# FNet mixing into a sigmoid-gated FFN: the first batch's transform grows with its rows, the Nyquist column travels as row 0 of G2, and weight conversions move within their iterations

## The chip, the cores and the metric

The kernel runs on one core of one Trainium2 chip. The metric is the device time of a whole execution in microseconds. Five engines work side by side, each with its own instruction stream in program order: TensorE (PE, with PEld for the loading of its stationary operand), VectorE (DVE), ScalarE (ACT), GpSimd (POOL) and SyncE (SP). SyncE is used to issue DMAs; ScalarE issues some as well, and an issue takes its turn among the engine's other instructions.

## The reference

An input x of 8 batches, 3008 rows and 256 features goes through a two-dimensional Fourier transform, of which the real part is kept. The result, seen as 24064 tokens of 256 features, goes through a gated feed-forward layer of 1536 hidden units.

```python
X = np.fft.fft(np.fft.fft(x, axis=1), axis=2).real      # (8, 3008, 256)
x = X.reshape(24064, 256)
gate = 1.0 / (1.0 + np.exp(-(x @ w_gate)))              # (256, 1536)
val = x @ w_val                                         # (256, 1536)
out = (gate * val) @ w_out                              # (1536, 256)
```

## The kernel before, in words

**Symmetry.** The host sends each batch as four groups of 126 x 6 rows (a row, its mirror, the row half a turn away and the mirror of that). `fold_ops` adds and subtracts these groups and mirrored features, so that a transform along the rows needs only cosine and sine tables `st` for a quarter of the frequencies, and one along the features only 128 columns. Batch 0 is folded on VectorE, the others on GpSimd, a few operations per iteration.

**Transform along the rows.** `half` sums, for one of two parities `blk` and one kind `what`, over the six row slices q: even q into a PSUM bank `ev`, odd q into `od`. ScalarE copies `ev` to `a`, and VectorE forms a + od and a - od, which go to places k and M - k of a row block. The kinds are pk (what 0, cosine part of features 0 to 127), qk (what 1, sine part of features 1 to 127) and ek (what 2, the feature 128, spread over all partitions). Batch 0 computes its own ek from a stationary operand `we`, which ScalarE fills with 128 copies of one column. For batches 1 to 7 the column comes by `e_load` (seven DMAs of x8), `e_fold`, `e_rows` and a trip through DRAM.

**Transform along the features.** It is merged into the weights. `merge` multiplies the table `dt` (256 x 256) with 256 columns of w_gate (g = 0) or w_val (g = 1): `ps` gives G1 (cosine rows) and G2 (127 sine rows), `pe` gives the column for feature 128, turned so that hidden units lie on partitions (`ge`). The weights are 64 bit floats; `weight_round` makes 32 bit floats of the raw words in six steps (L163 and L164 on ScalarE, L165, L166 and L168 on VectorE, L170 on GpSimd). Conversions are staged through `jobs`, numbered j; the first KEEP = 5 come ahead of the loop, the others three per two iterations. `forms` prepares w_out as seven combinations per pair of hidden blocks, a product of two by two blocks with seven multiplications.

**Main loop.** Frequencies 0 to 1504 are cut in 6 chunks of up to 256. For each batch, chunk and pair i of hidden blocks (6 pairs of 2 x 128) there are two iterations. In each, `front` computes pa (G1 x pk) and pb (G2 x qk) for gate and value, VectorE adds ge x ek to pa (ae, L326), and z = ae + pb and ae - pb (L329, L330) are the values at k and at its mirror. ScalarE applies the sigmoid (L495), `gate` multiplies gate and value (h, L341), GpSimd makes the sums sf (L343 to L347), and `back` does the second matrix product into four banks po, two pairs later. After the last pair of a chunk `finish` evacuates and stores through SyncE. An iteration ends with one entry of `later` and the entries of `side` (`at`, `split`): weight work in iterations 0 to 9, loads of the next batch, folds, row transforms.

**Order around the change.** The emission order is the order on each engine. An iteration emits front, gate of the iteration before, back, sigmoid, then the side work, in which `merge` comes ahead of `weight_round`. PSUM has eight banks: four in the rotating pool x (pa, pb, ps, pe, ev, od) and four for po. The raw words of the first five weights share three buffers; later ones lie in `mega`, in the place of batch 0's rows.

Of the kernel before, what the change touches and what calls it, by code (L numbers as in the profile page):

```python
# [38 lines left out]
NQ = 6  # L39
# [5 lines left out]
def kernel(  # L45
# [45 lines left out]
    def mm(o, l, r, start, stop):  # L91
        nc.tensor.matmul(o, l, r, start=start, stop=stop, skip_group_check=True)  # L92

    def bank(name):
        return psx.tile([P, 512], F32, name=name, tag="x")


# [7 lines left out]

    def load_x(b, nq):
        X[b] = xp.tile([NP, 4, NQ, D], F32, name="x4", tag="x4")
        for q in range(0, NQ, nq):
            rows(X[b][:, :, q : q + nq], xf[b, :, :, q : q + nq])

    dt = const.tile([P, 2, D], F32, name="dt")
    st = const.tile([NP, 2, NQ, NE + NO], F32, name="st")
    wf = const.tile([P, NPR, 7, P], F32, name="wf")
    G1 = const.tile([P, 2, F], F32, name="G1")
    G2 = const.tile([HD - 1, 2, F], F32, name="G2")
    ge = const.tile([P, 2, NFT], F32, name="ge")

    x8 = const.tile([NP, B - 1, 4, NQ], F32, name="x8")
    ed = dram.tile([B - 1, NK], F32, name="ed")

    def load_tables():
        for t in range(2):
            for cs in (slice(0, NE), slice(NE, NE + NO)):
                rows(st[:, t, :, cs], stab[:, t, :, cs])


    jobs = [(w, c) for c in range(NPR) for w in range(3)]
    RAW, WS = {}, {}
    mega = []
    KEEP = 5  # L130
# [21 lines left out]
            RAW[j] = raw  # L152
            nc.sync.dma_start(out=raw.rearrange("p c f w -> p c (f w)"), in_=src.bitcast(I32))

    def weight_round(j):
        if j not in RAW:
            return
        raw = RAW.pop(j)
        lo, hi = raw[:, :, :, 0], raw[:, :, :, 1]
        ws = WS[j]  # L160
        wi = ws.bitcast(I32)
        ts = nc.vector.tensor_scalar
        nc.scalar.activation(ws, hi.bitcast(F32), AF.Abs)  # L163
        nc.scalar.activation(lo, lo.bitcast(U32), AF.Copy, scale=2.0 ** -29)  # L164
        ts(out=ws, in0=ws, scalar1=2.0 ** -15, scalar2=HUGE, op0=ALU.max, op1=ALU.min)  # L165
        ts(out=wi, in0=wi, scalar1=3, scalar2=0x3FFFFFF8, op0=ALU.logical_shift_left,  # L166
           op1=ALU.bitwise_and)
# [4 lines left out]
    def weight_use(j):  # L172
        w, c = jobs[j]
        (forms(WS.pop(j), c) if w == 2 else merge(WS.pop(j), w, c))
# [31 lines left out]
    def fold_ops(b, eng, nq):  # L206
        x4 = X.pop(b)
        tt = eng.tensor_tensor
        ops = []

        def point(i, j, q):
            tt(x4[:, i, q, 1:D], x4[:, i, q, 1:D], x4[:, j, q, D - 1 : 0 : -1], op=ALU.add)

        def first(i, j, q):
            tt(x4[:, i, q, 0], x4[:, i, q, 0], x4[:, j, q, 0], op=ALU.add)

        def feat(v, r, q):
# [12 lines left out]
        if b:  # L230

            for n, group in enumerate(zip(*[kind(q) for q in qs])):
                ops += [f for fs in group for f in fs]
                if n < 2:
                    ops.append(lambda n=n: first(2 * n, 2 * n + 1, slice(0, NQ)))
        else:

            for q in qs:
                for n, fs in enumerate(kind(q)):
                    ops += fs  # L240
                    if n < 2:
                        ops.append(lambda n=n, q=q: first(2 * n, 2 * n + 1, q))
# [12 lines left out]
    def half(w, d, blk, sn, rows):  # L255

        c0, n = ((0, NE), (NE, NO))[blk]
        ev, od = bank("ev")[0:rows, 0:n], bank("od")[0:rows, 0:n]
        for o, par in ((ev, 0), (od, 1)):
            for q in range(par, NQ, 2):  # L260
                mm(o, w(q), st[:, int(sn), q, c0 : c0 + n], q == par, q >= NQ - 2)
        a = evp.tile([P, NE], F32, name="a", tag="a")[0:rows, 0:n]
        nc.scalar.copy(a, ev)
# [7 lines left out]
        return then  # L271

    def seq_start(b):
        PQE[b] = (pqp.tile([P, NK], F32, name="pk", tag="pk"),
                  pqp.tile([HD - 1, NK], F32, name="qk", tag="qk"),
                  pqp.tile([P, NK], F32, name="ek", tag="ek"))
        if b:
            nc.sync.dma_start(out=PQE[b][2], in_=ed[b - 1 : b, :].to_broadcast([P, NK]))

    def seq_group(b, blk, what):  # L280
        return half(lambda q: W[b, blk][what][:, q, :], PQE[b][what], blk, what == 1,
                    HD - 1 if what == 1 else P)


    ER = []

    def e_load():
        for b in range(1, B):
            nc.scalar.dma_start(out=x8[:, b - 1], in_=xf[b, :, :, :, HD : HD + 1])
# [8 lines left out]
    def e_rows(blk):  # L298
        if not blk:
            ER.append(cp.tile([B - 1, NK], F32, name="er", tag="c7"))  # L300
        return half(lambda q: x8[:, :, 1 + 2 * blk, q], ER[0], blk, False, B - 1)

    def e_out():
        nc.scalar.dma_start(out=ed, in_=ER.pop())
# [162 lines left out]
    at(i0 + 1, lambda: load_x(1, 3), e_load)  # L467

    for b in range(B - 1):
        s0 = b * per  # L470
        if b:
            at(s0 + 1, lambda b=b: load_x(b + 1, 3))
        f0, g0, gs = (s0 + 9, s0 + 36, 8) if b else (i0 + 9, i0 + 36, 7)

        def folds(f0=f0, b=b):
# [12 lines left out]
    for i in range(2 * len(pairs)):  # L488
# [69 lines left out]
```

## Time and profile before

| What | Value |
|---|---|
| Time, median of 3 runs | 2076.5 us (2075.3 to 2077.08) |
| Span of the profiled execution | 2072.8 us |
| PE busy, share of the span | 2023.2 us, 98% |
| DVE, POOL, ACT busy | 1750.4, 1316.3, 502.2 us |
| First main-loop matmul (pa) | 49.38 us |
| First ae on VectorE | 57.05 us |
| PE busy from 160 to 2063 us | 1902.25 of 1903 us |
| DMA in all | 70.96 MB, of it 0.39 MB in 21552 packets on ScalarE's queue |

Times in a profile count from the first instruction. Busy time of an engine is the sum of its instructions; the rest is waiting. Matmuls in 32 bit floats appear as two records each, so "pa x4" is two products of 128 x 128 by 256. A row of the chain of waits names the instruction that was running when nothing else could have ended the program earlier; a row of order of time has start, duration, engine, line, operation, output and inputs, and in brackets how long the engine had been idle and what released it. The granted clock is that of TensorE, 1.00 for full speed.

### The profile page before, as it was taken

How to read it: one execution, taken by the hardware profiler on the slowest of the kernel's cores; microseconds unless marked ns; L12 is line 12 of the kernel's file. 1: busy time of each engine (PE TensorE's matmuls, PEld its weight loads, DVE VectorE, ACT ScalarE, POOL GpSimd, SP SyncE). 2: the span in 40 equal slices, each digit the busy share in tenths (PEclk: the TensorE clock that was granted, in tenths of full speed). 3: DMA queues.
4: the chain of work that ended last, by engine and by line, in shares of the span. 5: the costliest groups of instructions: out<-in, count | busy, mean ns of one | idle time of the engine just before them, and what ended most of it. 6: DMA issues, size and time to landing. Idle time of an engine off the chain costs nothing.

```text
span 2072.8 us, 27549 instructions
## 1 busy us (share of the span) xinstructions
PE 2023.2 (98%) x9264; PEld 1757.7 (85%) x9264; DVE 1750.4 (84%) x3233; ACT 502.2 (24%) x892; POOL 1316.3 (64%) x1627
## 2 busy tenths in 40 slices
PE   7789999999999999999999999999999999999998
PEld 4677789888898888988899888988889888898887
DVE  4768878998889977998789987899879988798887
ACT  2422222222222222222222222222222222222222
POOL 0546944696558944687556974579545885565654
PEclk9899999999999999999999999999999999999999
DMA  8341000300020100301003000120003010000001
GB/s 207 109 82 12 11 27 16 75 26 11 18 69 14 32 16 11 71 19 27 11 11 80 26 11 11 32 58 26 16 16 71 13 32 11 11 16 15 11 16 24
DMA packets 142281, 70.96 MB, mean 34 GB/s; under 512 B 124783, under 2 KB 128063, under 8 KB 142142
## 3 DMA queue, kind: packets, MB, share of 16 engines
q1 hardware_dynamic: 120590, 68.83, 14.0%
q10 hardware_dynamic: 21552, 0.39, 0.7%
q8 instruction: 74, 1.21, 0.2%
q14 instruction: 65, 0.53, 0.1%
HBM read 44.50 MB, written 24.68 MB: 33 GB/s over the span
## 4 chain that ended last, share of the span: by engine, by line
PE 72%; POOL 14%; DVE 6%; issue 2%; ACTq 1%; ACT 0%; DVEq 0%; POOLq 0%
PE po L92 31%; PE pa L92 18%; PE pb L92 17%; PE ev L92 3%; PE od L92 3%; POOL sf L346 2%; POOL sf L345 2%; POOL sf L343 2%; POOL sf L347 2%; DVE ae L326 2%; DVE h L341 1%; POOL x L218 1%; POOL x L226 1%; POOL x L219 1%; DVE z L330 1%
## 5 line engine op out<-in xcount | busy, mean ns | idle before, releaser
L495 ACT ACTIVATE z<-z 128x512 f32<-128x512 f32 (+1 forms) x576 | 358.5, 622 | 1330.6 <-DVE z L330 1330.6
L326 DVE SCALAR_TENSOR_TENSOR ae<-ek,ge,pa 128x256 f32<-128x256 f32 (+1 forms) x1152 | 489.9, 466 | 194.1 <-PE pa L92 191.0
L92 PE MATMUL pa<-pk,G 128*128 128x256 f32 (+1 forms) x2304 | 587.4, 377 | 9.9 <-ACT G L187 5.2
L92 PE MATMUL pb<-qk,G 127*128 127x256 f32 (+1 forms) x2304 | 585.6, 376 | 0.4 <-DVE z L330 0.4
L92 PE MATMUL po<-sf,wf 128*128 128x256 f32 (+1 forms) x2304 | 537.4, 375 | 0.6
L92 PEld LDWEIGHTS pa<-pk,G 128*128 128x128 f32 x2304 | 438.2, 191 | 69.1 <-ACT G L187 7.4
L92 PEld LDWEIGHTS pb<-qk,G 127*128 127x128 f32 x2304 | 439.0, 191 | 53.2 <-PE pa L92 0.7
L92 PEld LDWEIGHTS po<-sf,wf 128*128 128x128 f32 x2304 | 435.5, 190 | 55.7 <-POOL sf L347 3.5
L345 POOL TENSOR_TENSOR sf<-h 128x256 f32<-128x256 f32 (+1 forms) x288 | 212.6, 738 | 400.0 <-DVE h L341 400.0
L341 DVE TENSOR_TENSOR h<-z 128x512 f32<-128x512 f32 (+1 forms) x576 | 447.0, 776 | 11.4 <-ACT z L495 11.4
L329 DVE TENSOR_TENSOR z<-ae,pb 128x512 f32<-128x512 f32 (+1 forms) x576 | 390.1, 677 | 61.1 <-DVE ae L326 1.4
L92 PE MATMUL po<-h,wf 128*128 128x256 f32 (+1 forms) x1728 | 416.4, 377 | 8.8 <-ACT c L370 8.8
L330 DVE TENSOR_TENSOR z<-ae,pb 128x512 f32<-128x512 f32 (+1 forms) x576 | 386.3, 671 | 0.0
L92 PEld LDWEIGHTS po<-h,wf 128*128 128x128 f32 x1728 | 329.6, 191 | 49.0 <-ACT c L370 9.2
L343 POOL TENSOR_TENSOR sf<-h 128x256 f32<-128x256 f32 (+1 forms) x288 | 219.0, 760 | 225.5 <-DVE h L341 222.3
L346 POOL TENSOR_TENSOR sf<-sf,h 128x256 f32<-128x256 f32 (+1 forms) x288 | 214.6, 745 | 22.6
L347 POOL TENSOR_TENSOR sf<-h,sf 128x256 f32<-128x256 f32 (+1 forms) x288 | 213.5, 741 | 22.6
L382 ACT COPY c<-po 128x512 f32<-128x512 f32 (+1 forms) x144 | 78.4, 580 | 64.4 <-PE po L92 64.3
L389 DVE STREAM_TRANSPOSE os<-c 128x256 f32<-128x256 f32 x192 | 83.8, 438 | 0.0
L92 PE MATMUL ev<-st,x 126*128 126x377 f32 (+5 forms) x204 | 71.9, 489 | 6.0 <-ACT ge L189 6.0
L411 POOL TENSOR_TENSOR c<-c 128x512 f32<-128x512 f32 (+1 forms) x47 | 73.6, 1566 | 0.0
L92 PE MATMUL od<-st,x 126*128 126x377 f32 (+5 forms) x204 | 70.1, 479 | 0.0
(80 smaller groups left out, 745.1 us busy)
## 6 DMA issues: line engine op xcount, KB each, us to landing
x<-in_xf_dram SPq DMA_DIRECT2D x14, 1344.0 KB
out_dram<-os SPq DMA_DIRECT2D x288, 64.0 KB
out_dram<-os SPq DMA_DIRECT2D x96, 56.0 KB
ek<-ed SPq DMA_DIRECT2D x7, 752.5 KB
x<-in_xf_dram SPq DMA_DIRECT2D x3, 896.0 KB
mega<-in_moe_w_out_dram SPq DMA_DIRECT2D x5, 512.0 KB
x<-in_xf_dram SPq DMA_DIRECT2D x14, 168.0 KB
mega<-in_moe_w_gate_dram SPq DMA_DIRECT2D x4, 512.0 KB
```

What stands on the lines that cost most here:

```text
L92: nc.tensor.matmul(o, l, r, start=start, stop=stop, skip_group_check=True)
L326: nc.vector.scalar_tensor_tensor(out=ae[:, g], in0=ek[:, ks], scalar=ge[:, g, f : f + 1], in1=pa[:, g], op0=ALU.mult, op1=ALU.add)
L329: nc.vector.tensor_tensor(z[:, :, 0], ae, pb, op=ALU.add)
L330: nc.vector.tensor_tensor(z[:, :, 1, ::-1], ae, pb, op=ALU.subtract)
L341: nc.vector.tensor_tensor(h[:, fh], z[:, 0], z[:, 1], op=ALU.mult)
L343: tt(s[:, 2], h[:, 0, 0], h[:, 0, 1], op=ALU.subtract)
L345: tt(s[:, 0], h[:, 0, 1], h[:, 1, 1], op=ALU.add)
L346: tt(s[:, 1], s[:, 0], h[:, 0, 0], op=ALU.subtract)
L347: tt(s[:, 3], h[:, 1, 0], s[:, 1], op=ALU.subtract)
L382: nc.scalar.copy(t[:, 2 * j : 2 * j + 2, 0:n], PO[j][:, :, 0:n])
L389: nc.vector.transpose(os_[:, s, 0:nb, h, :], t[:, slot, 0 : nb * TB])
L495: nc.scalar.activation(z[:, 0], z[:, 0], AF.Sigmoid)
```

## The change

The change has these parts.

- Batch 0's rows and the cosine table arrive in alternating slices of two q; weights and the sine table come after them. Each slice is folded, and then its share of four cosine groups is summed; these groups hold eight PSUM banks at once, four of them the po banks. `half` therefore gives back its summing, its copy and its placing apart.
- The column for feature 128 becomes row 0 of G2: `merge` uses 128 rows of the table for its second half. A DMA turns this row of 128 hidden units into a column of `ge`. So that row 0 adds nothing to pb, row 0 of qk must be zero; `feat` sets its source to zero.
- `we` goes; a broadcast view of the column is the stationary operand.
- A conversion is cut in two: `weight_parts` (ScalarE) ahead of the iteration's sigmoid, `weight_join` (VectorE, GpSimd) in the side work. The order of `jobs` changes, so that w_out's part for a pair comes later, and the merges of g = 0 and g = 1 take one iteration each, with one and two conversions beside them.
- `e_load` issues from SyncE.

```diff
--- before.py
+++ after.py
-    def bank(name):
+    def bank(name, other=None):
+        if other is not None:
+            return pso.tile([P, 512], F32, name=name, tag=f"po{other}")
         return psx.tile([P, 512], F32, name=name, tag="x")
...
     def load_x(b, nq):
         X[b] = xp.tile([NP, 4, NQ, D], F32, name="x4", tag="x4")
-        for q in range(0, NQ, nq):
-            rows(X[b][:, :, q : q + nq], xf[b, :, :, q : q + nq])
+        return [lambda q=q: rows(X[b][:, :, q : q + nq], xf[b, :, :, q : q + nq])
+                for q in range(0, NQ, nq)]
...
-    G2 = const.tile([HD - 1, 2, F], F32, name="G2")
+    G2 = const.tile([P, 2, F], F32, name="G2")
...
-    def load_tables():
-        for t in range(2):
-            for cs in (slice(0, NE), slice(NE, NE + NO)):
-                rows(st[:, t, :, cs], stab[:, t, :, cs])
+    def load_table(t, nq):
+        return [lambda q=q: rows(st[:, t, q : q + nq], stab[:, t, q : q + nq])
+                for q in range(0, NQ, nq)]
...
-    jobs = [(w, c) for c in range(NPR) for w in range(3)]
+    jobs = [(w, c - (w == 2)) for c in range(NPR + 1) for w in range(3)
+            if (c if w == 2 else c < NPR)]
...
-    def weight_round(j):
+    def weight_parts(j):
+        if j in RAW:
+            raw, ws = RAW[j], WS[j]
+            lo, hi = raw[:, :, :, 0], raw[:, :, :, 1]
+            nc.scalar.activation(ws, hi.bitcast(F32), AF.Abs)
+            nc.scalar.activation(lo, lo.bitcast(U32), AF.Copy, scale=2.0 ** -29)
+
+    def weight_join(j):
...
-        nc.scalar.activation(ws, hi.bitcast(F32), AF.Abs)
-        nc.scalar.activation(lo, lo.bitcast(U32), AF.Copy, scale=2.0 ** -29)
         ts(out=ws, in0=ws, scalar1=2.0 ** -15, scalar2=HUGE, op0=ALU.max, op1=ALU.min)
...
-    def merge(ws, g, c):
+    def merge(ws, g, c, other):
         cs = slice(c * WC, (c + 1) * WC)
-        ps, pe = bank("ps"), bank("pe")
-        for t in range(2):
-            mm(ps[:, 0:WC], dt[:, t, 0:HD], ws[:, t, :], t == 0, t == 1)
-        for t in range(2):
-            mm(ps[0 : HD - 1, WC : 2 * WC], dt[:, t, HD + 1 : D], ws[:, t, :], False, t == 1)
-        for i in range(WC // P):
+        ps = bank("ps", other)
+        for h in range(2):
             for t in range(2):
-                mm(pe[:, i : i + 1], ws[:, t, i * P : (i + 1) * P], dt[:, t, HD : HD + 1],
-                   t == 0, t == 1)
+                mm(ps[:, h * WC : (h + 1) * WC], dt[:, t, h * HD : (h + 1) * HD], ws[:, t, :],
+                   h == 0 and t == 0, t == 1)
+        nc.scalar.copy(G2[:, g, cs], ps[:, WC : 2 * WC])
         nc.scalar.copy(G1[:, g, cs], ps[:, 0:WC])
-        nc.scalar.copy(G2[:, g, cs], ps[0 : HD - 1, WC : 2 * WC])
-        nc.scalar.copy(ge[:, g, c * WC // P : (c + 1) * WC // P], pe[:, 0 : WC // P])
+        for f in range(c * WC // P, (c + 1) * WC // P):
+            (nc.sync if c else nc.scalar).dma_start(
+                out=ge[:, g, f : f + 1], in_=G2[0:1, g, f * P : (f + 1) * P])
...
         def feat(v, r, q):
-            tt(r[:, q, 0 : HD - 1], v[:, q, 1:HD], v[:, q, D - 1 : HD : -1], op=ALU.subtract)
+            eng.memset(r[:, q, 0:1], 0.0)
+            tt(r[:, q, 1:HD], v[:, q, 1:HD], v[:, q, D - 1 : HD : -1], op=ALU.subtract)
...
-            W[b, blk] = (v[:, :, 0:HD], r[:, :, 0 : HD - 1])
-            if b == 0:
-                we = cp.tile([NP, NQ, P], F32, name="we", tag="c7")
-                ops.append(lambda we=we, v=v: nc.scalar.copy(
-                    we, v[:, :, HD : HD + 1].to_broadcast([NP, NQ, P])))
-                W[b, blk] += (we,)
+            W[b, blk] = (v[:, :, 0:HD], r[:, :, 0:HD],
+                         v[:, :, HD : HD + 1].to_broadcast([NP, NQ, P]))
...
     def e_load():
         for b in range(1, B):
-            nc.scalar.dma_start(out=x8[:, b - 1], in_=xf[b, :, :, :, HD : HD + 1])
+            nc.sync.dma_start(out=x8[:, b - 1], in_=xf[b, :, :, :, HD : HD + 1])
...
+    for fx, ft in zip(load_x(0, 2), load_table(0, 2)):
+        fx()
+        ft()
     for j in range(2):
         weight_load(j)
-    load_x(0, 2)
-    load_tables()
+    for f in load_table(1, 2):
+        f()
     for j in range(2, KEEP):
         weight_load(j)
-    for j in range(2):
-        weight_round(j)
-    for f in fold_ops(0, nc.vector, 2):
+    seq_start(0)
+    folds0 = fold_ops(0, nc.vector, 2)
+    cos = [seq_group(0, blk, what, (2 * blk, 2 * blk + 1) if what else None)
+           for what in (0, 2) for blk in range(2)]
+    for i, f in enumerate(folds0):
         f()
-    for j in range(2):
-        weight_use(j)
-    seq_start(0)
-    for blk, what in ((0, 0), (0, 2), (1, 0), (1, 2), (0, 1), (1, 1)):
-        seq_group(0, blk, what)()
+        for sums, _ in cos:
+            sums(2 * i, 2 * i + 1)
+    weight_parts(0)
+    cos[0][1]()()
+    weight_parts(1)
+    weight_join(0)
+    cos[1][1]()()
+    weight_join(1)
+    for _, then in cos[2:]:
+        then()()
+    sin = [seq_group(0, blk, 1) for blk in range(2)]
+    for i in range(NQ // 2):
+        for sums, _ in sin:
+            sums(2 * i, 2 * i + 1)
+        if i < 2:
+            weight_use(i, i)
     for j in range(2, KEEP):
-        weight_round(j)
-    weight_use(2)
+        weight_parts(j)
+    for _, then in sin:
+        then()()
+    for j in range(2, KEEP):
+        weight_join(j)
...
-    def weight_step(j):
-        weight_round(j)
-        if j + 3 < len(jobs):
-            weight_load(j + 3)
+    def weight_step(i, *js):
+        for j in js:
+            pre.setdefault(i, []).append(lambda j=j: weight_parts(j))
+            at(i, lambda j=j: weight_join(j))
+            if j + 3 < len(jobs):
+                at(i, lambda j=j: weight_load(j + 3))
+    pre = {}
     for c in range(1, NPR):
         i = 2 * (c - 1)
-        at(i, lambda c=c: weight_use(3 * c), lambda c=c: weight_step(3 * c + 2))
-        at(i + 1, lambda c=c: weight_use(3 * c + 1), lambda c=c: weight_use(3 * c + 2))
+        j = 3 * c - 1
+        at(i, lambda j=j: weight_use(j))
+        at(i + 1, lambda j=j: weight_use(j + 1))
+        at(i + (c > 1), lambda j=j: weight_use(j + 2))
         if c + 1 < NPR:
-            at(i, lambda c=c: weight_step(3 * c + 3))
-            at(i + 1, lambda c=c: weight_step(3 * c + 4))
+            weight_step(i, j + 3)
+            weight_step(i + 1, j + 4, j + 5)
+        else:
+            weight_step(i, j + 3)
+            at(i + 1, lambda j=j: weight_use(j + 3))
...
         if i >= 4:
             back(i // 2 - 2, i % 2)
+        for f in pre.pop(i, []):
+            f()
         z = fresh[2]
         nc.scalar.activation(z[:, 0], z[:, 0], AF.Sigmoid)
```

More of the change, by code (lines that the diff above doesn't have):

```diff
@@ L153, in weight_load @@
             nc.sync.dma_start(out=raw.rearrange("p c f w -> p c (f w)"), in_=src.bitcast(I32))
-    def weight_round(j):
+    def weight_parts(j):
[5 more added lines that the diff above has]
+    def weight_join(j):
         if j not in RAW:
             return
-        raw = RAW.pop(j)
+        raw, ws = RAW.pop(j), WS[j]
         lo, hi = raw[:, :, :, 0], raw[:, :, :, 1]
-        ws = WS[j]
         wi = ws.bitcast(I32)
         ts = nc.vector.tensor_scalar
-        nc.scalar.activation(ws, hi.bitcast(F32), AF.Abs)
-        nc.scalar.activation(lo, lo.bitcast(U32), AF.Copy, scale=2.0 ** -29)
         ts(out=ws, in0=ws, scalar1=2.0 ** -15, scalar2=HUGE, op0=ALU.max, op1=ALU.min)
@@ L170, in weight_round, with weight_use @@
         nc.gpsimd.tensor_tensor(wi, wi, lo, op=ALU.add)
-    def weight_use(j):
+    def weight_use(j, other=None):
         w, c = jobs[j]
-        (forms(WS.pop(j), c) if w == 2 else merge(WS.pop(j), w, c))
-    def merge(ws, g, c):
-        cs = slice(c * WC, (c + 1) * WC)
-        ps, pe = bank("ps"), bank("pe")
-        for t in range(2):
-            mm(ps[:, 0:WC], dt[:, t, 0:HD], ws[:, t, :], t == 0, t == 1)
-        for t in range(2):
-            mm(ps[0 : HD - 1, WC : 2 * WC], dt[:, t, HD + 1 : D], ws[:, t, :], False, t == 1)
-        for i in range(WC // P):
+        if w == 2:
+            forms(WS.pop(j), c)
+        else:
+            merge(WS.pop(j), w, c, other)
+    def merge(ws, g, c, other):
+        cs = slice(c * WC, (c + 1) * WC)
+        ps = bank("ps", other)
+        for h in range(2):
             for t in range(2):
-                mm(pe[:, i : i + 1], ws[:, t, i * P : (i + 1) * P], dt[:, t, HD : HD + 1],
-                   t == 0, t == 1)
+                mm(ps[:, h * WC : (h + 1) * WC], dt[:, t, h * HD : (h + 1) * HD], ws[:, t, :],
+                   h == 0 and t == 0, t == 1)
+        nc.scalar.copy(G2[:, g, cs], ps[:, WC : 2 * WC])
         nc.scalar.copy(G1[:, g, cs], ps[:, 0:WC])
-        nc.scalar.copy(G2[:, g, cs], ps[0 : HD - 1, WC : 2 * WC])
-        nc.scalar.copy(ge[:, g, c * WC // P : (c + 1) * WC // P], pe[:, 0 : WC // P])
+        for f in range(c * WC // P, (c + 1) * WC // P):
+            (nc.sync if c else nc.scalar).dma_start(
+                out=ge[:, g, f : f + 1], in_=G2[0:1, g, f * P : (f + 1) * P])
     def forms(ws, c):
@@ L238, in fold_ops, with half, sums, places @@
             for q in qs:
+                part = []
                 for n, fs in enumerate(kind(q)):
-                    ops += fs
+                    part += fs
                     if n < 2:
-                        ops.append(lambda n=n, q=q: first(2 * n, 2 * n + 1, q))
+                        part.append(lambda n=n, q=q: first(2 * n, 2 * n + 1, q))
+                ops.append(lambda part=part: [f() for f in part])
         for blk, (v, r) in enumerate(parts):
-            W[b, blk] = (v[:, :, 0:HD], r[:, :, 0 : HD - 1])
-            if b == 0:
-                we = cp.tile([NP, NQ, P], F32, name="we", tag="c7")
-                ops.append(lambda we=we, v=v: nc.scalar.copy(
-                    we, v[:, :, HD : HD + 1].to_broadcast([NP, NQ, P])))
-                W[b, blk] += (we,)
+            W[b, blk] = (v[:, :, 0:HD], r[:, :, 0:HD],
+                         v[:, :, HD : HD + 1].to_broadcast([NP, NQ, P]))
         return ops
     PQE = {}
-    def half(w, d, blk, sn, rows):
+    def half(w, d, blk, sn, rows, other=None):
         c0, n = ((0, NE), (NE, NO))[blk]
[L258 to L263, printed above, removed]
+        ev, od = [bank(name, other and other[i])[0:rows, 0:n] for i, name in enumerate(("ev", "od"))]
+        def sums(*qs):
+            for q in sorted(qs, key=lambda q: q % 2):
+                mm((ev, od)[q % 2], w(q), st[:, int(sn), q, c0 : c0 + n], q < 2, q >= NQ - 2)
         def then():
+            a = evp.tile([P, NE], F32, name="a", tag="a")[0:rows, 0:n]
+            nc.scalar.copy(a, ev)
+            return lambda: places(a)
+        def places(a):
             nc.vector.tensor_tensor(d[:, blk : blk + 2 * n - 1 : 2], a, od, op=ALU.add)
@@ L270, in then, with whole @@
                                     op=ALU.subtract)
-        return then
+        return sums, then
+    def whole(sums, then):
+        sums(*range(NQ))
+        return then()
     def seq_start(b):
         PQE[b] = (pqp.tile([P, NK], F32, name="pk", tag="pk"),
-                  pqp.tile([HD - 1, NK], F32, name="qk", tag="qk"),
+                  pqp.tile([P, NK], F32, name="qk", tag="qk"),
                   pqp.tile([P, NK], F32, name="ek", tag="ek"))
@@ L278, in seq_start, with seq_group @@
             nc.sync.dma_start(out=PQE[b][2], in_=ed[b - 1 : b, :].to_broadcast([P, NK]))
-    def seq_group(b, blk, what):
-        return half(lambda q: W[b, blk][what][:, q, :], PQE[b][what], blk, what == 1,
-                    HD - 1 if what == 1 else P)
+    def seq_group(b, blk, what, other=None):
+        return half(lambda q: W[b, blk][what][:, q, :], PQE[b][what], blk, what == 1, P, other)
     ER = []
@@ L300, in e_rows @@
             ER.append(cp.tile([B - 1, NK], F32, name="er", tag="c7"))
-        return half(lambda q: x8[:, :, 1 + 2 * blk, q], ER[0], blk, False, B - 1)
+        return whole(*half(lambda q: x8[:, :, 1 + 2 * blk, q], ER[0], blk, False, B - 1))
     def e_out():
@@ L452, in split @@
         at(i, lambda: at(i + 1, f(*args)))
-    def weight_step(j):
-        weight_round(j)
-        if j + 3 < len(jobs):
-            weight_load(j + 3)
+    def weight_step(i, *js):
[5 more added lines that the diff above has]
+    pre = {}
     for c in range(1, NPR):
         i = 2 * (c - 1)
-        at(i, lambda c=c: weight_use(3 * c), lambda c=c: weight_step(3 * c + 2))
-        at(i + 1, lambda c=c: weight_use(3 * c + 1), lambda c=c: weight_use(3 * c + 2))
+        j = 3 * c - 1
+        at(i, lambda j=j: weight_use(j))
+        at(i + 1, lambda j=j: weight_use(j + 1))
+        at(i + (c > 1), lambda j=j: weight_use(j + 2))
         if c + 1 < NPR:
-            at(i, lambda c=c: weight_step(3 * c + 3))
-            at(i + 1, lambda c=c: weight_step(3 * c + 4))
+            weight_step(i, j + 3)
+            weight_step(i + 1, j + 4, j + 5)
+        else:
+            weight_step(i, j + 3)
+            at(i + 1, lambda j=j: weight_use(j + 3))
     i0 = 2 * NPR
-    at(i0 + 1, lambda: load_x(1, 3), e_load)
+    at(i0 + 1, lambda: [f() for f in load_x(1, 3)], e_load)
     for b in range(B - 1):
@@ L471 @@
         if b:
-            at(s0 + 1, lambda b=b: load_x(b + 1, 3))
+            at(s0 + 1, lambda b=b: [f() for f in load_x(b + 1, 3)])
         f0, g0, gs = (s0 + 9, s0 + 36, 8) if b else (i0 + 9, i0 + 36, 7)
@@ L480 @@
         for j in range(4):
-            split(g0 + gs * j, seq_group, b + 1, j // 2, j % 2)
+            split(g0 + gs * j, lambda b=b, j=j: whole(*seq_group(b + 1, j // 2, j % 2)))
     at(i0 + 22, e_fold)
```

## The prediction

> **What bounds the kernel now.** I read the page first, then the busy time by stretches of 10 us, then order of time where the stretches show holes, and the waits in those places. The page says that TensorE is nearly everything:
>
> ```profile
> PE 2023.2 (98%) x9264; PEld 1757.7 (85%) x9264; DVE 1750.4 (84%) x3233; ACT 502.2 (24%) x892; POOL 1316.3 (64%) x1627
> ```
>
> So 49.6 us (2072.8 - 2023.2) are open idleness of PE, and busy time at half clock comes on top. The stretches say where (columns: stretch, length, busy time of PE, PEld, DVE, ACT, POOL, granted clock, DMA share, GB/s):
>
> ```profile
> 20.00:30.00 10.00, 5.17 (x11) 3.03 (x12) 4.77 (x12) 3.25 (x9) 0.00 (x0) 0.66 1.10 234
> ...
> 50.00:60.00 10.00, 5.20 (x16) 3.75 (x15) 9.00 (x15) 2.78 (x6) 5.32 (x7) 0.78 0.48 158
> ...
> 80.00:90.00 10.00, 6.11 (x15) 4.44 (x15) 7.92 (x14) 2.86 (x8) 5.93 (x8) 0.66 0.33 107
> ...
> 150.00:160.00 10.00, 1.20 (x6) 0.74 (x5) 0.00 (x0) 0.70 (x2) 0.00 (x0) 0.73 0.75 5
> ```
>
> The reader sees three separate places: the start (to 57 us), the first chunk while weights are converted (57 to 130), and a hole at 150. After 160 PE is busy 1902.25 of 1903 us to the tail. The hole, in order of time:
>
> ```profile
> 142.54 16.72 ACTq L289 DMA_DIRECT2D x<-in_xf_dram  x7
> ...
> 159.30 0.37 ACT L370 COPY c<-po 128x256 f32<-128x256 f32 x1 [16.16 <-issue]
> ...
> 159.73 3.08 PE L92 MATMUL po<-h,wf 128*128 128x256 f32 x6 [8.80 <-ACT c L370]
> ```
>
> Seven DMA issues (e_load) hold ScalarE's instruction stream for 16.72 us; its evacuation copies and sigmoids queue behind them, and PE runs dry. In the first chunk the waits between 57 and 160 us, and VectorE's groups between 57 and 129.5 us, read:
>
> ```profile
> DVE mega L165 <- ACT mega L163: 15.2, 8, 3.2
> ```
>
> ```profile
> L166 DVE TENSOR_SCALAR mega<-mega 128x512 int32<-128x512 int32 x13 | 10.8, 830 | 0.4
> ...
> L165 DVE TENSOR_SCALAR mega<-mega 128x512 f32<-128x512 f32 x13 | 6.5, 499 | 17.7 <-ACT mega L163 15.2 <-POOL sf L347 2.5
> ```
>
> VectorE sets the pace there, and 15.2 us of it are a wait for ScalarE's Abs, which stands behind sigmoid and copies in program order. Last, one place in the steady part where PE waits for GpSimd (chain of waits, batch 1; five later batches show the same step of 1.56 us):
>
> ```profile
> 461.64 1.22 POOL sf L346
> 462.87 0.07 issue
> 462.94 0.74 POOL sf L347
> 463.68 0.04 issue
> 463.72 1.56 PE po L92 x6
> ```
>
> Six such records take 1.30 us when nothing holds them, so GpSimd has no slack left here, once per batch.
>
> **What the Trainium skill says.** DMA: Bandwidth & Descriptors, Rules for kernel authors: a DMA whose last dimension is not contiguous becomes one descriptor per element. The page's queue 10 with 21552 packets for 0.39 MB agrees. The same page, Anatomy of one DMA, puts a fixed part of about 2.0 us on a DMA, measured on the gpsimd path; no row here isolates it. SBUF — State Buffer, Who interferes with whom: a tensor_scalar in two-port mode and GpSimd exclude each other for a whole instruction. The trace agrees: L166 takes 0.43 us alone and 1.40 beside the 1.28 us add of L170. TensorE: Matmul & The Clock Gate, What's actually happening: half clock after an idle window of about 3.4 us, and again full after about as long busy. The trace has clock 0.50 from 22 to 28 us after an idle stretch.
>
> **The change part by part.**
>
> *e_load to SyncE's queue.* Removed from ScalarE: 16.72 us. PE's last matmul before the hole ends at about 150.8 and the next starts at 159.73: 9.0 us. Then PE is slow: po x6 3.08 for 1.30, pa x4 1.71 for 0.86, pb 1.05 for 0.86, together 2.8. Gain 11.8 us. Behind the seven issues on SyncE stand only the stores of chunk 0, due some 8 iterations of 3.24 us after them, against 16.7 us; x8 itself is read 21 iterations later. Cost 0.
>
> *Conversions.* The two ScalarE steps (1.2 us per weight) move ahead of the iteration's sigmoid, so VectorE finds them done after its product h. Before, from the first ae (57.05) to PE's front of iteration 10 (129.5) pass 72.5 us. VectorE's own work in it is ae 8.7, z 6.9 and 6.8, h 6.2, L165 6.5, L166 10.8, L168 9.0 and 0.7: 55.6 us, with overlaps of about 0.09 us per instruction counted twice. TensorE's work there is 10 fronts of 1.73, six half backs (3 x 3.03) and 10 ps of 1.73: 43.7, so VectorE stays the bound. Of the 17 us between 72.5 and 55.6, the 15.2 us wait goes; I give back some 2 us, because the conversion now starts right after h, when GpSimd begins its sf subtractions (0.73 us each), and the locks become likelier. Gain 13 us, 72.5 to about 59.5. Bounds: 3 if every lock costs a full sf operation more, 17 if VectorE never waits.
>
> *merge.* Eight pe matmul records per merge go (0.79 us of PE, 12 times), also a copy of 0.17 us; PE is not the bound there, so they count inside the 13 us. New: the ge column comes by a DMA of 128 single elements after the G2 copy. Queued behind its issue on SyncE are weight loads that wait anyway for L170 of the same iteration. Who waits for it is the first ae of the next column pair. For g = 1: sigmoid 0.63, copy 0.27, issue about 0.4 (L153's issues take 0.37 to 0.47), flight about 2.0 by the DMA page: 3.3 us after z; VectorE meanwhile has h 0.6 and two conversions of 1.9 and 2.6: 5.1. Hidden, with 1.8 us to spare; a weight load of 512 KB ahead in the ring could eat that (512 KB at the 370 GB/s of 40 to 42 us is 1.4). I take 0; the bad end, 2 us for each of five pairs, is 10.
>
> *Start.* The 10.5 MB of x, tables and five weights land between 2 and 42 us: 263 GB/s. The first x slice is then there at 2 + 1.29 MB / 263 = 6.9 (the same sum with the weights ahead gives 10.9 for before, whose first fold starts at 10.99). Each further slice of x with its cosines is 1.79 MB, 6.8 us: x at 6.9, 13.7, 20.5. A slice folds in 4.5 us: 11.4, 18.2, 25.0. Its 16 matmul records at 0.317 (1.90 for 6) take 5.1, the first slice 3.4 more at half clock: cosine sums end near 30, where before they end at 41.5. Then data bound again: w0, w1 by 27.4, sines by 36, w2 to w4 by 42.5. Sine sums and two merges are 7.6 + 3.5 of PE after the first banks come free at about 31: 42.2. Parts of the fifth weight precede the sine copies on ScalarE: 42.5 + 1.25, copy 0.47, four places of 0.55: 46.5. Three joins as before, 6.6 (50.57 to 57.14): first ae at 53.1 against 57.05. Gain 4 us; ends 0 (loads stall on the third raw buffer) and 6. The two we copies, 1.56 us, go; the stationary operand is read with step 0, which no trace here shows: I take no cost, and the 24 records concerned would cost at worst their own 191 ns twice, 5 us, partly hidden by loads.
>
> *Zero row.* On batch 0 three pairs of memsets on VectorE, under 0.5 us, beside DMA waits. On batches 1 to 7 GpSimd gets 6 memsets per batch, of 126x2 elements. Nearest rows: 126x6 adds with a step of 0.16 us, memset 128x1 of 0.10. Five of six stand ahead of the pinch shown, where every us lands on PE: 5 x 0.12 = 0.6 us, in six batches 3.5 us. Low end 0, high end 5 x 0.62 x 6 = 18 when each also meets a lock as long as one 0.43 us VectorE operation. 127 to 128 rows in pb and the sine groups change no duration.
>
> Sum: -11.8 - 13 - 4 + 3.5 = -25.3; 2076.5 becomes 2051.
>
> **Rivals.** (a) The wait for Abs is replaced: locks against sf, or the ge DMA behind weight loads. For it: L166 already averages 830 ns where 430 is free. Against: h and conversions cover the column's 3.3 us. First chunk gains 3: 2076.5 - 11.8 - 3 - 4 + 3.5 = 2061. (b) Everything hides: VectorE at its floor and free memsets. For it: GpSimd's step of 0.04 us between independent operations. Against: the pinch has no slack. 2076.5 - 11.8 - 17 - 4 = 2044. (c) Slower: 42 memsets at 0.62 (26), nothing gained at the start or in the first chunk, only the hole closed: 2076.5 - 11.8 + 26 = 2091. For it: GpSimd lies on the chain in six batches. Against: both memset rows are far below 0.62.
>
> **How the numbers follow.** Forecast 0.62, (a) 0.18, (b) 0.17, (c) 0.03. The range 2043 to 2062 takes in (a) and (b) and leaves out (c) and the corners of unknown costs. Only (c) is not faster by 4 us (0.2%); a hundredth is for a result within 0.2%. So faster 0.96, same 0.01, slower 0.03.
>
> **What would show it.** No hole at 150, and seven issues of 2.2 us on SyncE. First ae near 53; iteration 10's front near 113; the wait of L165 for L163 almost gone, L166 still near 0.8. ae never released by a ge DMA. Memsets of 0.1 us on GpSimd, and the step of 1.56 us near 464 grown by half a microsecond in each of six batches. I am wrong if VectorE's idle time in the first chunk only changes its name, if the first ae comes after 56, or if the part after the first chunk grows by more than 6 us.

## The result and the profile after

| | Before | After |
|---|---|---|
| Time, median (lowest to highest) | 2076.61 us (2075.3 to 2077.08) | 2045.67 us (2044.44 to 2047.17) |
| Ratio, 95% interval | | 0.9852 (0.9835 to 0.9869) |
| Span of the profiled execution | 2072.8 us | 2045.2 us |

The change saves 30.9 us; 2051 was forecast, a saving of 25.3, with a range of 2043 to 2062. The profiled execution of the changed kernel is the slowest of its four, and its span is only 27.6 us shorter; a second profile of the same kernel (run e9) has a span of 2042.2 us. Both are used below, each by its name. Line numbers have moved: in the kernel after, ae is L343, z L346 and L347, h L358, the matmuls L93, the sums sf L360 to L364, and the steps of a conversion L164, L165, L174, L175, L177 and L179.

The page of the kernel after, engines:

```profile
PE 2002.3 (98%) x9168; PEld 1741.9 (85%) x9168; DVE 1751.7 (86%) x3239; ACT 500.1 (24%) x878; POOL 1323.7 (65%) x1669
```

Shares say little again: PE is at 98% as before. Idle PE is now 42.9 us in place of 49.6; most of the saving is busy time that went (20.9 us), among it matmuls at half clock and the pe products. The same four stretches of 10 us as before (length, busy time of PE, PEld, DVE, ACT, POOL, granted clock, DMA share, GB/s):

```profile
20.00:30.00 10.00, 7.66 (x25) 4.31 (x24) 5.17 (x14) 1.61 (x4) 0.00 (x0) 1.00 1.05 253
50.00:60.00 10.00, 8.24 (x27) 5.80 (x25) 9.59 (x16) 1.43 (x2) 5.95 (x7) 0.71 0.01 5
80.00:90.00 10.00, 9.04 (x42) 7.63 (x41) 9.65 (x17) 5.33 (x12) 8.14 (x9) 1.00 0.54 156
150.00:160.00 10.00, 10.00 (x49) 8.79 (x48) 9.53 (x19) 1.89 (x3) 6.47 (x9) 1.00 0.12 26
```

The stretch at 150 is full. At 80 VectorE is busy 9.65 of 10 us, where it was 7.92: it no longer waits. The issues of x8 in order of time, kernel after, SyncE:

```profile
120.86 24.96 SPq L306 DMA_DIRECT2D x<-in_xf_dram  x7
154.67 1.88 SPq L416 DMA_DIRECT2D out_dram<-os  x4
```

They now fill 25 us of SyncE's stream, longer than the 16.72 on ScalarE: one of the seven takes 13.2 us, and their median is 2.16 us (2.23 on ScalarE). The first stores come 8.9 us after them, and the profile lists no wait of PE from 130 to 2040 us, so nothing suffers.

VectorE's waits from 56 to 119 us of the kernel after are all that is left in the first chunk:

```profile
DVE ae L343 <- PE pa L93: 2.6, 2, 1.8
DVE ae L343 <- DMA ge<-G: 0.8, 1, 0.8
DVE z L346 <- PE pb L93: 0.6, 1, 0.6
```

The 15.2 us for Abs are gone; once, by 0.8 us, an ae waited for the ge column. VectorE's groups between 55.51 and 112.84 us in e9, the second profile:

```profile
L177 DVE SCALAR_TENSOR_TENSOR mega<-mega 128x512 int32<-128x512 int32 x13 | 11.6, 891 | 0.4
L175 DVE TENSOR_SCALAR mega<-mega 128x512 int32<-128x512 int32 x13 | 10.3, 793 | 0.4
...
L174 DVE TENSOR_SCALAR mega<-mega 128x512 f32<-128x512 f32 x13 | 6.3, 485 | 0.0
```

L175, the former L166, is still near 0.8 us; L177, the former L168, grew from 692 to 891 ns, and h from 684 to 743: 13 x 0.20 + 9 x 0.06 = 3.1 us more in these two rows. They read as the lock waits for which the prediction gave back 2 us: in e9 an L177 with nothing on GpSimd beside it takes 0.69 us (at 63.75), and one that starts while GpSimd runs L363 takes 1.10 (at 70.98). Other rows shrank, and VectorE's busy time in the whole stretch rose by 1.7 us, from 52.14 (57.05 to 129.5 us, before) to 53.87. Last the pinch, the place where PE waits for GpSimd once per batch, in the chain of waits, kernel after, batch 1:

```profile
435.12 1.23 POOL sf L363
436.34 0.07 issue
436.41 0.73 POOL sf L364
437.14 0.04 issue
437.19 1.56 PE po L93 x6
```

It is as long as before, 1.56 us, although five memsets now stand ahead of it; so it is in the five later batches.

### The profile page after: what moved, and what is told of

It is laid out like the page before. It is cut to its first block, busy times and chain, and to the rows that moved or that the text cites. A ratio compares the mean times of both kernels' runs of the same rounds, so it can differ in the third digit from the quotient of the medians.

```text
span 2045.2 us, 27431 instructions
## 1 busy us (share of the span) xinstructions
PE 2002.3 (98%) x9168; PEld 1741.9 (85%) x9168; DVE 1751.7 (86%) x3239; ACT 500.1 (24%) x878; POOL 1323.7 (65%) x1669
## 2 busy tenths in 40 slices
DMA packets 143530, 70.98 MB, mean 35 GB/s; under 512 B 128299, under 2 KB 128555, under 8 KB 143390
## 3 DMA queue, kind: packets, MB, share of 16 engines
q1 hardware_dynamic: 142528, 68.93, 14.8%
## 4 chain that ended last, share of the span: by engine, by line
PE 84%; DVE 8%; POOL 4%; DMA 2%; issue 1%; ACT 0%; SPq 0%; DVEq 0%; ACTq 0%; POOLq 0%
PE po L93 37%; PE pa L93 21%; PE pb L93 20%; PE ev L93 3%; PE od L93 3%; DVE ae L343 2%; DVE h L358 2%; DVE z L347 2%; DMA st<-in_stab_dram 1%; DVE z L346 1%; POOL x L230 1%; POOL x L229 1%; POOL sf L363 1%; POOL sf L362 1%; DVE os L406 0%
## 5 line engine op out<-in xcount | busy, mean ns | idle before, releaser
L343 DVE SCALAR_TENSOR_TENSOR ae<-ek,ge,pa 128x256 f32<-128x256 f32 (+1 forms) x1152 | 489.5, 465 | 193.0 <-PE pa L93 189.5
L93 PE MATMUL pa<-pk,G 128*128 128x256 f32 (+1 forms) x2304 | 583.9, 375 | 14.6 <-ACT G L196 11.1
L93 PE MATMUL pb<-qk,G 128*128 128x256 f32 (+1 forms) x2304 | 584.7, 376 | 0.4 <-DVE qk L280 0.4
L93 PE MATMUL po<-sf,wf 128*128 128x256 f32 (+1 forms) x2304 | 537.2, 375 | 0.8
L93 PEld LDWEIGHTS pa<-pk,G 128*128 128x128 f32 x2304 | 437.1, 190 | 74.1 <-ACT G L196 13.5
L93 PEld LDWEIGHTS po<-sf,wf 128*128 128x128 f32 x2304 | 436.2, 190 | 55.6 <-POOL sf L364 4.5
L93 PEld LDWEIGHTS pb<-qk,G 128*128 128x128 f32 x2304 | 439.3, 191 | 51.4 <-DVE qk L280 0.8
L358 DVE TENSOR_TENSOR h<-z 128x512 f32<-128x512 f32 (+1 forms) x576 | 449.3, 780 | 0.0
L346 DVE TENSOR_TENSOR z<-ae,pb 128x512 f32<-128x512 f32 (+1 forms) x576 | 389.8, 677 | 62.0 <-DVE ae L343 1.8
L93 PE MATMUL po<-h,wf 128*128 128x256 f32 (+1 forms) x1728 | 413.4, 375 | 0.0
L347 DVE TENSOR_TENSOR z<-ae,pb 128x512 f32<-128x512 f32 (+1 forms) x576 | 385.7, 670 | 0.0
L93 PEld LDWEIGHTS po<-h,wf 128*128 128x128 f32 x1728 | 329.4, 191 | 37.5
L360 POOL TENSOR_TENSOR sf<-h 128x256 f32<-128x256 f32 (+1 forms) x288 | 218.5, 759 | 210.8 <-DVE h L358 209.3
L364 POOL TENSOR_TENSOR sf<-h,sf 128x256 f32<-128x256 f32 (+1 forms) x288 | 215.0, 746 | 22.6
L363 POOL TENSOR_TENSOR sf<-sf,h 128x256 f32<-128x256 f32 (+1 forms) x288 | 214.7, 746 | 22.6
L93 PE MATMUL ev<-st,x 126*128 126x377 f32 (+3 forms) x216 | 77.5, 485 | 15.6 <-DVE x L230 14.6
L93 PE MATMUL od<-st,x 126*128 126x377 f32 (+3 forms) x216 | 76.8, 482 | 0.0
```

The source lines that it names most:

```text
L343: nc.vector.scalar_tensor_tensor(out=ae[:, g], in0=ek[:, ks], scalar=ge[:, g, f : f + 1], in1=pa[:, g], op0=ALU.mult, op1=ALU.add)
L346: nc.vector.tensor_tensor(z[:, :, 0], ae, pb, op=ALU.add)
L347: nc.vector.tensor_tensor(z[:, :, 1, ::-1], ae, pb, op=ALU.subtract)
L358: nc.vector.tensor_tensor(h[:, fh], z[:, 0], z[:, 1], op=ALU.mult)
L360: tt(s[:, 2], h[:, 0, 0], h[:, 0, 1], op=ALU.subtract)
L363: tt(s[:, 1], s[:, 0], h[:, 0, 0], op=ALU.subtract)
```

## The experiments

**Where the saving comes from.** Four kernels part the change. e1 is the kernel before with one word changed:

```diff
-            nc.scalar.dma_start(out=x8[:, b - 1], in_=xf[b, :, :, :, HD : HD + 1])
+            nc.sync.dma_start(out=x8[:, b - 1], in_=xf[b, :, :, :, HD : HD + 1])
```

> The kernel before with nothing but the seven DMA issues of e_load moved from ScalarE to SyncE. My account (three gains that add: the hole 11.8 us, the order of the conversions some 14, the start 1): 2076.6 - 11.8 = 2065, no idle stretch of PE at 150 us, the first chunk as before (iteration 10's first pa at 129.5). Rival (SyncE blocks loads and stores as much as ScalarE was blocked, the gain comes from the rest): 2072 or more, with a wait for stores or loads in place of the hole.

Measured: 2065.02 us, ratio 0.994 (0.9924 to 0.9957); the kernel before, run beside it, took 2077.26, so 12.2 us less. PE in its profile is full there:

```profile
150.00:160.00 10.00, 10.00 (x48) 8.76 (x48) 8.34 (x16) 2.45 (x6) 6.72 (x8) 1.00 0.73 5
```

And the wait of the first chunk is still there (waits between 50 and 130 us, e1):

```profile
DVE mega L165 <- ACT mega L163: 17.5, 9, 3.2
```

The hole is one gain by itself, and it is as large as the idle stretch with the half-clock stretch after it.

e2 is the changed kernel with the ScalarE steps back in the side work:

```diff
-            pre.setdefault(i, []).append(lambda j=j: weight_parts(j))
-            at(i, lambda j=j: weight_join(j))
+            at(i, lambda j=j: weight_parts(j), lambda j=j: weight_join(j))
```

> The changed kernel, but the two ScalarE steps of a conversion stand again in the side work, behind sigmoid and copies, directly ahead of the VectorE steps. My account: the wait of VectorE for Abs comes back (13 to 15 us in all), time 2045.7 + 13 = 2059. Rival (the 96 pe matmuls and copies that went are what made the first chunk shorter): at most 3 us more, 2049.

Measured: 2061.29 us, ratio 0.9923 (0.9908 to 0.9938), 15.6 us more than the changed kernel. The wait is back under its new line numbers (VectorE's waits between 55 and 127 us, e2):

```profile
DVE mega L174 <- ACT mega L164: 14.8, 9, 3.6
```

From the first ae to that of iteration 12, the first of the second chunk, pass 81.18 us in e2, 80.08 in the kernel before and 63.81 in e9. So the place of two ScalarE instructions in their stream is worth some 15 us; what else changed in this chunk, the removed pe products and the new order of jobs, did not shorten it by itself. e8 puts the question the other way, with pe back in place of the DMAs:

```diff
-        for f in range(c * WC // P, (c + 1) * WC // P):
-            (nc.sync if c else nc.scalar).dma_start(
-                out=ge[:, g, f : f + 1], in_=G2[0:1, g, f * P : (f + 1) * P])
+        pe = bank("pe", None if other is None else other + 2)
+        for i in range(WC // P):
+            for t in range(2):
+                mm(pe[:, i : i + 1], ws[:, t, i * P : (i + 1) * P], dt[:, t, HD : HD + 1],
+                   t == 0, t == 1)
+        nc.scalar.copy(ge[:, g, c * WC // P : (c + 1) * WC // P], pe[:, 0 : WC // P])
```

> The changed kernel with ge computed again by eight matmul records per merge and a ScalarE copy, in place of the two DMAs. Theory V (VectorE sets the pace of the first chunk): the 0.79 us of PE per merge hide, time 2045 to 2048. Theory T (what was removed from TensorE is what the first chunk gained): 10 x 0.79 us come back, 2053.

Measured: 2044.65 us, ratio 0.9853 (0.9838 to 0.9867), the changed kernel's ratio. From the first ae to that of iteration 12 pass 64.20 us, against 63.81 in e9: in the first chunk the DMA column neither brings nor costs anything that can be measured. For the whole time e8 is not a clean test, since it also takes the four ge issues off ScalarE at the start. Against e6 below, which leaves them out too and ran beside it (2042.94 to 2044.03 us, e8 2044.21 to 2045.55), it is 1.1 us slower, so the pe products may cost that much; the intervals of the two ratios overlap.

e3 gives the changed kernel the old start (weights first, table by column blocks, all folds, then group after group):

```diff
-    for fx, ft in zip(load_x(0, 2), load_table(0, 2)):
...
+    for f in fold_ops(0, nc.vector, 2):
+        f()
+    for j in range(2):
+        weight_use(j)
+    seq_start(0)
+    for blk, what in ((0, 0), (0, 2), (1, 0), (1, 2), (0, 1), (1, 1)):
+        whole(*seq_group(0, blk, what))()
```

> The changed kernel with the start of the kernel before: weights first, table by column blocks, all folds, then one group after the other in the four rotating banks. My account: first ae in the two profiles differs by 0.85 us only, so the time is 2046 to 2048, with the first ae near 57. Rival (the growth by slices carries several us, seen in the time and not in the first ae): 2050 or more.

Measured: 2048.12 us, ratio 0.986 (0.9846 to 0.9875), 2.4 us more than the changed kernel. The edge is between the two expectations: the first ae of the old start lies at 57.05, 58.49 and 59.35 us in three profiles (before, e1, e3), that of the new one at 56.20, 55.12 and 55.51 (after, e2, e9). The growth by slices is worth 1 to 4 us at the first ae, and 2.4 us in the time.

**Why the start gained less than forecast.** ScalarE's stream in the kernel after shows what held it (order of time):

```profile
42.26 1.79 ACTq L198 DMA_DIRECT2D ge<-G  x2
...
44.10 0.66 ACT L164 ACTIVATE ws<-raw 128x512 f32<-128x512 f32 x1 [1.60 <-issue]
...
46.84 0.64 ACT L165 ACTIVATE raw<-raw 128x512 int32<-128x512 uint32 x1
47.38 0.84 ACT L276 COPY a<-ev 128x377 f32<-128x377 f32 x2
```

The sine sums end at 44.35, but their copies start at 47.38: six conversion steps stand ahead, and ahead of those two ge issues of 1.79 us together. VectorE waits for the copies (its waits from 40 to 57 us, kernel after):

```profile
DVE qk L280 <- ACT a L276: 11.5, 1, 11.5
```

e4, e5 and e6 take these apart:

```diff
-    for j in range(2, KEEP):
-        weight_parts(j)
     for _, then in sin:
         then()()
+    for j in range(2, KEEP):
+        weight_parts(j)
...
-            (nc.sync if c else nc.scalar).dma_start(
+            nc.sync.dma_start(
```

e4 has both hunks, e5 the first, e6 the second.

> The changed kernel with the copies of the two sine groups ahead of the ScalarE steps of weights 2 to 4, and the first four ge columns issued from SyncE. My account (ScalarE's program order holds the start, not the data): sine copies near 44, first ae near 53 for 56.2, time 2042.5. Rival (the start is bound by the data of the fifth weight, or by the three joins and the reload of raw buffers): first ae within 0.5 us of 56.2, time 2045 to 2046.

> The changed kernel with only the sine copies ahead of the ScalarE steps of weights 2 to 4; the first four ge columns still issue from ScalarE. In the changed kernel these issues hold ScalarE until 44.05, just when the sine sums end, so the copies would follow at once. Theory P (program order of the conversion steps is the cause): nearly all of the gain of the pair, 2042.5. Theory Q (the 3.0 us of DMA issues on ScalarE are): less than half of it, 2044 or more.

> The changed kernel with only the first four ge columns issued from SyncE. Theory P: the conversion steps start up to 1.8 us earlier and still stand ahead of the copies, 2044 to 2045.5. Theory Q: nearly the whole gain of the pair, 2042.5.

| Kernel | Time, us | Ratio (interval) | First ae, us |
|---|---|---|---|
| after (e9: 2046.07) | 2045.67 | 0.9852 (0.9835 to 0.9869) | 56.20 (e9: 55.51) |
| e4, both | 2042.05 | 0.983 (0.9816 to 0.9845) | 52.08 |
| e5, copies first | 2043.11 | 0.9845 (0.9829 to 0.9862) | 53.43 |
| e6, ge on SyncE | 2043.52 | 0.9847 (0.9832 to 0.9861) | 54.97 |

The second sine copy and the first ae in e4 (order of time), and what VectorE waits for there in place of ScalarE:

```profile
44.00 0.47 ACT L276 COPY a<-ev 128x376 f32<-128x376 f32 x1 [0.79 <-PE ev L93]
...
52.08 0.87 DVE L343 SCALAR_TENSOR_TENSOR ae<-ek,ge,pa 128x256 f32<-128x256 f32 x2
```

```profile
DVE qk L280 <- PE od L93: 6.7, 2, 6.4
```

Program order on ScalarE held the start, not the data. The first ae by itself differs by up to 1.1 us between profiles of one start (56.20 in after, 55.12 in e2), in part because the sine sums do not always end at the same time. Counted from the end of these sums, it comes after 11.32 to 11.85 us in e2, e9 and after, 8.56 in e5, 10.16 in e6 and 7.53 in e4. The copies bring 2.8 to 3.3 us, the issues 1.2 to 1.7, both 3.8 to 4.3, about their sum. Neither theory P nor Q, each of which gave one cause nearly everything, was right; the order of the copies is the larger part. e4 is the fastest kernel of this study: its runs (2041.12 to 2042.33 us) lie below all eight of the changed kernel (2044.27 to 2047.44). Its ratio's interval still touches that of the changed kernel, and those of e5 and e6 overlap it, so for these the first ae after the end of the sums is the better witness.

**The memsets.** e7 repeats the memset five times, e10 leaves it out on GpSimd:

```diff
-            eng.memset(r[:, q, 0:1], 0.0)
+            if eng is nc.vector:
+                eng.memset(r[:, q, 0:1], 0.0)
```

> The changed kernel with each memset of feat five times in a row (168 more on GpSimd, 24 more on VectorE for batch 0). A memset advances GpSimd by 0.06 us. Theory A (the wait of the following operation for a VectorE lock swallows it): 20 more ahead of each pinch are 1.2 us, of which the locks swallow a part; at most 0.5 us per batch is left, time 2046 to 2049, and in the trace the first operation after the memsets is shorter. Theory B (GpSimd has no slack in the fold phase, as the prediction had it): 6 batches x 1.2 us, 2053 and a matmul group at the pinch longer by 1.2 us.

> The changed kernel without the memsets on GpSimd (batches 1 to 7; row 0 of qk is then not zero and adds to pb). If the following operation's lock wait swallows a single memset, as the profile of the changed kernel suggests (stretched operations 1.13 to 1.17 for 1.17 to 1.20 us), within 0.5 us of the changed kernel beside it. If each of the five memsets ahead of a pinch costs its step of 0.06 us: 6 x 0.3 = 1.8 us less. The prediction's term: 3.5 us less.

e7: 2066.34 us, ratio 0.9957 (0.9943 to 0.9972), more than either theory said. Its batches follow each other by 248.0 us (pinch at 438.61, next at 686.63), those of e9 by 244.40. A repeated memset of the same place advances GpSimd by 0.16 us, not 0.06: 4 x 0.16 x 5 = 3.2 us ahead of a pinch, and 3.6 are lost per batch. At this first pinch some 1.4 us of it is PE at half clock behind its wait: the six records take 2.93 us for 1.56, with a granted clock of 0.50 from 439 to 441.3. Waits of PE in e7, from 130 us on:

```profile
PE po L93 <- POOL sf L367: 12.2, 6, 2.0
PE po L93 <- POOL sf L368: 2.6, 6, 0.4
```

So GpSimd has indeed no slack there, as theory B and the prediction had it. e10: 2044.72 us, ratio 0.9845 (0.9832 to 0.9859), against 2046.07 and 0.9851 (0.9838 to 0.9865) beside it; its batches follow by 244.27 us. One memset per feat costs 0.13 us per batch, about 0.8 us in all six. That is a rough figure: eight profiles with one and the same loop (after, e2 to e6, e8, e9) have 244.38 to 244.52 us per batch, averaged over five. But the 0.6 us of the prediction is excluded. What fits this is in the chains of the kernels before and after, batch 1:

```profile
458.95 1.14 POOL x L218
...
460.88 0.70 POOL sf L345
```

```profile
432.42 0.04 POOL x L228
432.46 1.10 POOL x L229
...
434.35 0.69 POOL sf L362
```

L229 behind the memset (L228) takes 1.10 us; its counterpart in the kernel before (L218) takes 1.14, and the sf operation behind both starts 2.88 us ahead of the pinch (order of time: 434.31 and 437.19; 460.84 and 463.72). An L229 that nothing holds takes 0.72. The stretched operation ends when it did before, as if released by VectorE, and a short instruction ahead of it mostly vanishes. That a lock does this is read from the durations, not tried by itself.

**Can the pinch be moved away?** Two kernels built on e4 shift the folds of batches 1 to 7 (e11) or 2 to 7 (e12):

```diff
-                at(f0 + j, f)
-        at(f0 - 1, folds)
+                at(f0 - 1 + j * 5 // 4, f)
+        at(f0 - 2, folds)
```

```diff
-        f0, g0, gs = (s0 + 9, s0 + 36, 8) if b else (i0 + 9, i0 + 36, 7)
+        f0, g0, gs = (s0 + 7, s0 + 36, 8) if b else (i0 + 9, i0 + 36, 7)
```

> The sine copies first and all ge columns from SyncE, and besides the 20 fold operations of batches 1 to 7 spread over 24 iterations in place of 20, from one iteration earlier. If GpSimd's backlog at the end of the folds is what holds PE once per batch (0.5 us in each of six), 3 us less than the version with the copies first: 4.1 + 3 us below the changed kernel beside it, and the matmul group of 1.56 us near 437 back at 1.30. If the pinch comes from chunk ends (the operations of finish) and not from the folds: no gain from the spreading, 4 us below the changed kernel.

> The sine copies first, all ge columns from SyncE, and the folds of batches 2 to 7 start two iterations earlier (s0 + 7 for s0 + 9), one per iteration as in the changed kernel. The run with the folds apart put four of the late fold pairs beside the second chunk's finish operations on GpSimd and lost 0.85 us per batch. Theory M (where folds meet the finish operations of a chunk sets the pinch): now the last fold ends before these begin, the 0.5 us per batch goes, 6 x 0.5 = 3 us below the version with the copies first (0.983 of the kernel before): 2039, ratio 0.9817. Rival (the backlog comes from the folds as such): the pinch only comes two iterations earlier, ratio 0.983.

e9 is the changed kernel once more, run beside e10 and e11:

> The changed kernel once more, as the partner of the two kernels beside it: 0.985 of the kernel before, 2045 to 2046.

e9 measured 2046.07 us, 0.9851 (0.9838 to 0.9865). e11: 2046.92 us, 0.9857 (0.9844 to 0.9871), 4.9 above e4. e12: 2044.43 us, 0.9844 (0.983 to 0.9857), 2.4 above e4. Both lost. The batches follow by 244.46 us in e4, 245.27 in e11 and 244.94 in e12. In e12 the pinch came earlier, at 425.48 for 431.33 in e4, when the last fold was only about to run (chain of waits, e12):

```profile
424.70 0.74 POOL sf L364
425.44 0.04 issue
425.48 1.56 PE po L93 x6
```

The first finish operation of the second chunk comes only after it (order of time, e12):

```profile
425.42 0.73 POOL L229 TENSOR_TENSOR x<-x 126x254 f32<-126x254 f32 x1
...
428.05 1.27 POOL L425 TENSOR_TENSOR c<-c 128x512 f32<-128x512 f32 x1
```

Theory M fell: the meeting with the second chunk's finish operations is not what makes the pinch. Whether it is what made e11 worse was not tried by itself. What spacing would remove the pinch stays open.

## Why the prediction was right, point by point

The range held the time, and every large step showed where it was put. The measured 2045.67 us lies nearer to rival (b), 2044, than to the forecast of 2051: as (b) said, the first chunk fell nearly to VectorE's own work and the memsets were nearly free, though GpSimd has no slack at the pinch, as the forecast said. The table takes the second profile, e9, whose span is 30.6 us shorter than that of before; the parts are differences of points in the two traces.

| Step | Forecast | Measured | From |
|---|---|---|---|
| Start, to the first ae | -4 | -1.5 | 57.05 to 55.51 |
| First chunk, first ae to that of iteration 12 | -13 | -16.3 | 80.08 to 63.81 |
| Hole | -11.8 | -11.8 | ae of iteration 12 to the first pinch: 326.59 to 314.77 |
| Zero row and the rest | +3.5 | -1.0 | first pinch to the end: 1609.08 to 1608.11 |
| Sum | -25.3 | -30.6 | |

The misses of the start (2.5 us too much) and of the first chunk (3.3 too little) nearly cancel, which is luck; the zero row's 4.5 remains. That the hole agrees to a tenth is in part luck too, since e1 alone gave 12.2.

- *Hole.* Right in place and size. The seven issues were to take 2.2 us each on SyncE; one takes 13.2, the others 2.0 on average. Nothing queued on SyncE minded the 25 us.
- *Conversions.* Right in mechanism, too small in size. The wait for Abs went whole, as e2 shows from the other side. To iteration 10, for which the 13 us were forecast, VectorE takes 57.3 us (55.51 to 112.84) where I left it 59.5; 15.1 us went, and 1.2 more up to iteration 12. The term that was mis-sized is the time given back. 72.5 - 15.2 is already 57.3, so in the end nothing was given back: VectorE's busy time rose by 1.7 us, but the wait of 2.5 us for GpSimd (L165 for L347) that I left in place went as well. The "17 us between 72.5 and 55.6" was also too little, because the 55.6 counts overlaps twice: VectorE is busy 52.14 us there and idle 20.3.
- *One profile against another.* In the profiled run after, PE idled 2.05 us ahead of iteration 10 and then ran at half clock (0.50 from 114 to 116 us, pb x4 1.91 us for 1.03); in e9 the wait was 1.20 us and the clock stayed. From the first ae to that of iteration 12 pass 66.23 us in the profile after and 63.81 in e9, 2.4 of the 3.0 us between the two spans; in e3 to e8, e10 and e12 it is 63.83 to 64.69. The length of the one wait does not settle it: both waits are shorter than the 3.4 us that the prediction quotes, and a wait of 2.04 us at 99 us in the profile after left the clock at 1.00.
- *merge.* Counted at nothing of its own: right for the first chunk, by e8. The ge DMA, which was not to release an ae at all, did so once, for 0.8 us (0.4 in e9). Rival (a) had no other support than the longer L177 and h.
- *Start.* The step that failed is "Parts of the fifth weight precede the sine copies on ScalarE: 42.5 + 1.25": I let the conversion steps of weights 2 and 3 run as their data landed. They stand behind the second merge's copies and the ge issues in program order, so all six run after 44.1 and the copies wait until 47.4. Also "issue about 0.4" was too low for these columns: the median is 0.59 us on either queue, and one on ScalarE took 1.28. The sine sums ended later too, at 44.35 us (43.85 in e9) for 42.2. By the prediction's own sign, "the first ae comes after 56", this part was wrong in the profile after (56.20) and at the edge in e9 (55.51).
- *Zero row.* The step "where every us lands on PE" holds (e7), but "5 x 0.12 = 0.6" per batch was too dear: 0.13 by e10, since a short memset mostly vanishes ahead of a stretched operation. So the step of 1.56 us did not grow by half a microsecond. The part from the pinch to the end is even 1.0 us shorter than before, memsets included: 0.4 in the five periods between pinches, no more than kernels with the same loop differ by (0.7 us in five), and 0.6 after the sixth pinch (386.69 us before and 386.75 in e1; 386.12 in e9 and at most 386.32 in after, e2 to e6 and e8). The step "127 to 128 rows in pb and the sine groups change no duration" may be part of it. From the sixth pinch on e9 gains evenly on the kernel before, 0.39 us in 355 us, where e1, with 127 rows too, gains 0.02. From the start of a pb to that of the next po, PE takes 866 ns on average in before and e1 and 863 to 865 in the kernels with 128 rows (some 60 groups each), from pa to pb 863 to 864 in all. That the row count does this was not tried by itself.
- *Skill.* DMA: Bandwidth & Descriptors, Rules for kernel authors, holds on SyncE as well: with one descriptor per element the seven x8 loads are 7 x 3024 = 21168, and SyncE's queue has 142528 packets for 120590 before, while ScalarE's fell from 21552 to 862. SBUF — State Buffer, Who interferes with whom, also says that a VectorE instruction with two SBUF inputs contends with a GpSimd instruction that reads SBUF; L177 is one, and its mean of 891 ns for 692 agrees.

## What to carry to other kernels

Look for instructions whose data are ready long before their turn: a preparation step on one engine, placed behind that engine's waiting work, made another engine wait here; moved ahead of the wait it gave 15 us. A DMA issue is an instruction of its engine, and one with many small pieces took microseconds here (2.2 us for 3024 elements); put it where nothing is queued behind it. To see whether an engine has slack, repeat the suspected cost several times: e7 showed at once that there is none, while the single memset nearly vanished beside a stretched operation.

## What was not expected of the hardware

Two ge columns of 128 elements took 1.20 us of ScalarE's stream in one pair of issues and 1.79 in another, against 0.37 us of SyncE for a weight of 512 KB. The seven x8 issues took 16.72 us on ScalarE, where no other load was in the queue, and 24.96 us on SyncE (24.18 in e1) behind 3 MB of rows in the same queue; whether these rows are the reason was not tried. A memset of 126x2 on GpSimd advanced its stream by 0.06 us ahead of an operation on other data, but by 0.16 us ahead of another memset of the same place.
